# Gate/value stage of a three-part fp32 layer: five token groups of 464 or 448 columns in place of six of 384

## The chip, the cores and the metric

The kernel runs on one core of one Trainium2 chip. The metric is the device time of one execution in microseconds, the median of several runs. The core has five engines with an instruction stream each: PE (TensorE, matrix products), DVE (VectorE), ACT (ScalarE), POOL (GpSimd) and SP (SyncE, which here only issues transfers). They meet through semaphores alone.

## The reference

Chunked attention, a feed-forward layer with a softmax-weighted activation and a layer norm, and a gated feed-forward layer follow each other over 4608 tokens of 512 features. The change lies in the third one:

```python
def _moe2_ref(x, w_gate, w_val, w_out):      # x: 4608 x 512
    g = x @ w_gate                           # 512 x 1536
    silu = g * (1.0 / (1.0 + np.exp(-g)))
    val = x @ w_val                          # 512 x 1536
    return (silu * val @ w_out)              # 1536 x 512
```

## The kernel before

Each fp32 product is made of three passes over operands that are split into a high and a low part (`PASSES`: high x high, high x low, low x high). The products of the third layer also use a seven-product scheme for 2 x 2 blocks (Strassen's, in Winograd's form), so each operand is first turned into seven blocks, by differences and sums, and each block is split into high and low.

The program has three stretches. Up to 517 us it computes attention and the first feed-forward layer; its last part, called the y stage here, writes y (the input x of the code above) tile by tile to DRAM. An outer step m covers 384 tokens (`TOK`), d one of four feature tiles; one (m, d) is 24 matmuls of 384 columns (L169). Beside it `w_tick` prepares the seven factors of each of the 12 pairs of gate and value blocks and spills them to DRAM (`ws_dram`, 1792 KB each).

The gate/value stage (517 to 1042 us) has NSG = 6 groups s of two halves of 384 tokens. For each group, 12 steps f. A step (`step`) runs seven `product`s of six matmuls (two k tiles x three passes; L862), with a block of y as the moving operand of 384 columns and a 128 x 128 piece of a factor block as the stationary one. ACT, DVE and POOL empty the four accumulators, apply the sigmoid and form `u` = silu(gate) x value, and SP stores it to `u_dram` during the next step. The seven blocks of y for the next group (`yk`, two buffers, yka and ykb) are made while the present group runs: `y_load` fetches y into `rawy`, and `y_units` gives a list of 8 differences on POOL and 14 splits (one ACT copy, one DVE subtraction each), which is worked off in small portions. For group 0 the portions are three units at a time from y tile (10, 0) on. Factor blocks come through a ring of three buffers (`ring_tile`, `w_load`), always three ahead; blocks 0 to 2 are kept in cached copies (`wc`, `cache_load`) for the groups before the last, and the list `orders` tells which steps use them.

In the last two groups the output weights are made ready too: `v_load` to `v_store` convert them, then for each of six pairs p `t_load` fetches two rows of blocks, `t_sums` makes four differences on POOL, and `t_split` makes the split copy `tw[p]` (ACT, then DVE).

The output stage (1042 to 1314 us) runs NU = 54 units n = (g, p), 9 groups g of 512 tokens and six p. A unit has 2 x 21 matmuls of 256 columns (L1082). For unit n, `x_load` fetches u, `x_sums` makes four sums on DVE, `x_high` copies the high part on ACT into `hl[n]` (in the three-buffer ring), `x_low` makes the low part on DVE. Unit n needs `hl[n]` and `tw[p]`. After p = 5 `evac` empties the accumulators pa, pb, pc, pd of each half i: ACT copies pa, DVE adds pb, POOL adds, DVE adds pc, and so on. The next group's matmuls write the same banks.

The scheduler is switched off for all of this (`manual_schedule`): every engine runs its instructions strictly in the order in which the code issues them.

Of the kernel before, what the change touches and what calls it, by code (L numbers as in the profile page):

```python
# [23 lines left out]
def attn_moe_moe2_kernel(  # L24
# [38 lines left out]
    y_dram = [  # L63
        [dram.tile([P, TOK], F32, tag=f"y{m}_{d}", name=f"y{m}_{d}") for d in range(KD)]
        for m in range(NG)
    ]
# [94 lines left out]
    def y_run(wB, i0, i1, ps, sb, ptags=("y",), stag="ysb", queue=nc.scalar):  # L161

        for i in range(i0, i1):
# [9 lines left out]
            if n == NY - 1:  # L173
                ysb = sb.tile([P, TOK], F32, tag=stag, name="ysb", bufs=2)
                nc.scalar.activation(out=ysb, in_=ys.pop(u), func=AF.Copy)  # L175
                queue.dma_start(out=y_dram[m][d], in_=ysb)
# [61 lines left out]
    with ExitStack() as ph1:  # L238
# [459 lines left out]
    SG = 2 * TOK  # L698
    NSG = NG // 2
# [5 lines left out]
    u_dram = [  # L705
        [dram.tile([P, 2, SG], F32, tag=f"u{s}_{p}", name=f"u{s}_{p}") for p in range(NFP)]
        for s in range(NSG)
    ]

    with ExitStack() as ph2:  # L710
# [7 lines left out]
        ry = cpa.tile([P, 11, TOK], F32, tag="ry", name="ry")  # L718
        rawy, tt = ry[:, 0:8].rearrange("p (a b) n -> p a b n", a=2), ry[:, 8:11]
        yk = {0: cpa.tile([P, NS, 2, 2, TOK], F32R, tag="yka", name="yka")}  # L720
# [9 lines left out]
        def yk_tile(s):  # L730
            x = "ab"[s % 2]
            return (cpa, cp)[s % 2].tile([P, NS, 2, 2, TOK], F32R, tag=f"yk{x}", name=f"yk{x}")
# [18 lines left out]
        def y_load(s):  # L751
            for kk in range(2):
                for i, (m, k) in enumerate(((0, 0), (1, 0), (0, 2), (1, 2))):
                    nc.sync.dma_start(out=rawy[:, kk, i], in_=y_dram[2 * s + m][k + kk])

        def y_units(s, kks=(0, 1)):
# [3 lines left out]
            dst, units = yk[s], []  # L760
            for kk in kks:
                b11, b12, b21, b22 = (rawy[:, kk, i] for i in range(4))
                t1, t2, t4 = (tt[:, i] for i in range(3))
# [55 lines left out]
        for m in range(1, NG):  # L819
            for d in range(KD):  # L820
# [8 lines left out]
                if k == END:  # L829
                    ahead_y = y_units(0)  # L830
                if last_m and d == 0:
                    stage_.close()
                    p2.close()
                    cp = ph2.enter_context(pool("cp"))
                    for i in range(2):
                        osb = cp.tile([P, TOK], F32, tag="osb", name="osb", bufs=2)
                    yk[1] = yk_tile(1)
                if last_m and d < RING:
                    w_load()
                for x in ahead_y[:3]:  # L840
                    x()
                ahead_y = ahead_y[3:]
# [6 lines left out]
        def cache_load(f):  # L849
# [318 lines left out]
```

## Time and profile before

| | |
|---|---|
| median of 3 runs | 1322.7 us (1322.65 to 1322.89) |
| profiled execution, its own time | 1322.13 us |
| its span in the profile | 1320.3 us |
| PE busy | 1297.1 us (98%) |
| DVE, ACT, POOL busy | 995.9 (75%), 620.4 (47%), 449.9 (34%) us |
| granted clock of TensorE | 0.999 |

The profile lists instructions with their line in the kernel, what they write and read, how often they ran, and how long. A matmul's recorded duration is longer than the distance to the next one, since matmuls overlap; the distance is what counts. The letters x4 behind a row mean that four neighbours of one kind are merged, and the duration then runs from the first one's start to the last one's end. Square brackets tell how long the engine had been idle and what released it. SPq is SP's queue of transfers.

### The profile page before, as it was taken

The numbers are of one execution on the slowest core, as the hardware profiler recorded it, in microseconds if no ns is written. First come the engines' busy times: TensorE is split into PE (matmuls) and PEld (weight loads), VectorE is DVE, ScalarE is ACT, GpSimd is POOL, SyncE is SP. The second block draws the span as 40 slices with busy tenths as digits, with TensorE's granted clock in tenths as the row PEclk, the third lists the DMA queues.
The fourth block names the chain that finished last, engine by engine and source line by source line (L and its number), as shares of the span: only waits on it lengthen the run. The fifth ranks groups of instructions, "written<-read, shape, count | busy, mean of one in ns | idle before, by whom it ended". The sixth has DMA issues, their size and how long they took to land. (4 is left out here: it accounts for less than half of the span.)

```text
span 1320.3 us, 26319 instructions
## 1 busy us (share of the span) xinstructions
PE 1297.1 (98%) x10058; PEld 1242.3 (94%) x10058; DVE 995.9 (75%) x1674; ACT 620.4 (47%) x1024; POOL 449.9 (34%) x601
## 2 busy tenths in 40 slices
PE   4999999999999999999999999999999999999998
PEld 3788888888999999999999999999999999999998
DVE  7788888886478774687777777787777788787875
ACT  5566666666566654243333433343333333334331
POOL 5455555554333441243333333433432000000111
PEclk9999999999999999999999999999999999999999
DMA  7355556575799997997888798767999544444441
GB/s 256 121 177 177 177 178 183 183 212 179 268 369 357 395 334 288 411 423 237 284 274 312 246 326 277 275 209 275 346 340 342 176 146 142 144 129 144 128 150 60
DMA packets 146830, 318.40 MB, mean 241 GB/s; under 512 B 11536, under 2 KB 94480, under 8 KB 139024
## 3 DMA queue, kind: packets, MB, share of 16 engines
q1 hardware_dynamic: 140368, 308.07, 67.5%
q10 hardware_dynamic: 6336, 8.65, 1.8%
q8 instruction: 79, 1.29, 0.4%
q14 instruction: 47, 0.39, 0.1%
HBM read 225.45 MB, written 91.23 MB: 240 GB/s over the span
## 5 line engine op out<-in xcount | busy, mean ns | idle before, releaser
L381 PE MATMUL h<-wA,x 128*128 128x512 f32 x864 | 216.6, 399 | 0.6 <-ACT x L361 0.3
L169 PE MATMUL y<-lnT,wB 128*128 128x384 f32 x1152 | 200.7, 334 | 0.6 <-ACT ysb L175 0.6
L169 PEld LDWEIGHTS y<-lnT,wB 128*128 128x128 f32 x1152 | 199.5, 188 | 0.9 <-ACT ysb L175 0.9
L381 PEld LDWEIGHTS h<-wA,x 128*128 128x128 f32 x864 | 156.8, 188 | 32.1 <-ACT x L361 1.5
L895 POOL TENSOR_TENSOR u<-u,p 128x384 f32<-128x384 f32 x72 | 73.1, 1015 | 217.6 <-DVE u L894 217.6
L897 ACT ACTIVATE u<-pa 128x384 f32<-128x384 f32 x72 | 35.4, 492 | 176.0 <-PE pa L862 176.0
L1092 POOL TENSOR_TENSOR work<-work 128x256 f32<-128x256 f32 x35 | 25.8, 747 | 249.2 <-DVE work L1092 231.1
L1001 ACT ACTIVATE hl<-ry 128x1792 fp32r<-128x1792 f32 x28 | 47.7, 1703 | 78.6 <-PE opd L1082 42.6
L898 DVE TENSOR_TENSOR u<-pa,u 128x384 f32<-128x384 f32 x72 | 40.1, 558 | 58.6 <-ACT u L897 58.1
L902 ACT ACTIVATE u<-p 128x384 f32<-128x384 f32 x72 | 37.9, 526 | 94.9 <-DVE p L901 94.9
L1001 ACT ACTIVATE hl<-work 128x1792 fp32r<-128x1792 f32 x26 | 44.3, 1704 | 73.8 <-PE opd L1082 40.0
L862 PE MATMUL pd<-ykb,ws 128*128 128x384 f32 x360 | 72.2, 334 | 0.0
L862 PE MATMUL pc<-ykb,ws 128*128 128x384 f32 x360 | 72.1, 334 | 0.0
L862 PE MATMUL pa<-ykb,ws 128*128 128x384 f32 x360 | 72.1, 334 | 0.0
L668 DVE TENSOR_TENSOR lnT<-lr,lnT 128x1536 fp32r<-128x1536 f32 x24 | 47.5, 1978 | 31.5 <-ACT lnT L667 26.9
L1006 DVE TENSOR_TENSOR hl<-ry,hl 128x1792 fp32r<-128x1792 f32 x28 | 56.6, 2022 | 14.8 <-ACT hl L1001 14.8
L862 PE MATMUL pa<-yka,ws 128*128 128x384 f32 x324 | 64.8, 334 | 0.0
L862 PE MATMUL pc<-yka,ws 128*128 128x384 f32 x324 | 64.8, 334 | 0.0
L862 PE MATMUL pd<-yka,ws 128*128 128x384 f32 x324 | 64.8, 334 | 0.0
L1006 DVE TENSOR_TENSOR hl<-work,hl 128x1792 fp32r<-128x1792 f32 x26 | 52.6, 2022 | 15.8 <-ACT hl L1001 15.8
L862 PEld LDWEIGHTS pd<-ykb,ws 128*128 128x128 f32 x360 | 63.2, 188 | 0.2 <-DVE u L894 0.2
L361 ACT ACTIVATE x<-so_ps 128x512 fp32r<-128x512 f32 x36 | 21.7, 602 | 88.7 <-PE so_ps L265 84.4
(148 smaller groups left out, 3212.4 us busy)
## 6 DMA issues: line engine op xcount, KB each, us to landing
ws<-ws SPq DMA_DIRECT2D x57, 1792.0 KB, 9.1
u<-u SPq DMA_DIRECT2D x72, 384.0 KB, 7.2
ln<-lt SPq DMA_DIRECT2D x72, 256.0 KB, 3.1
lr<-ln SPq DMA_DIRECT2D x24, 768.0 KB, 7.1
ry<-u SPq DMA_DIRECT2D x56, 256.0 KB, 3.2
work<-u SPq DMA_DIRECT2D x52, 256.0 KB, 3.2
ws<-shi SPq DMA_DIRECT2D x12, 896.0 KB, 9.4
qt<-in_q SPq DMA_DIRECT2D x36, 256.0 KB, 3.6
```

Of the source, the lines that this page charges most:

```text
L169: nc.tensor.matmul(ys[u], lhsT=wB[:, f, a, d * P:(d + 1) * P], rhs=lnT[m][:, b, f, :], start=(n == 0), stop=(n == NY - 1),)
L361: nc.scalar.activation(out=hi, in_=o, func=AF.Copy)
L381: nc.tensor.matmul(h[:, n * DM:(n + 1) * DM], lhsT=x[:, a, k, :], rhs=wA[:, n * KD + k, b, :], start=(j == 0), stop=(j == NH // 2 - 1),)
L668: nc.vector.tensor_tensor(out=lo, in0=x, in1=hi.bitcast(F32), op=ALU.subtract)
L862: nc.tensor.matmul(ps, lhsT=w[:, a, kk * P:(kk + 1) * P], rhs=y[:, b, kk], start=(first and n == 0), stop=(n == 5), skip_group_check=True,)
L895: nc.gpsimd.tensor_tensor(out=u3, in0=u3, in1=p5, op=ALU.add)
L897: nc.scalar.activation(out=sa, in_=psA, func=AF.Sigmoid)
L898: nc.vector.tensor_tensor(out=sa, in0=psA, in1=sa, op=ALU.mult)
L902: nc.scalar.activation(out=sb, in_=c12, func=AF.Sigmoid)
L1001: nc.scalar.activation(out=hl[n][:, 0], in_=xs[n][:, 1:8], func=AF.Copy)
L1006: nc.vector.tensor_tensor(out=hl[n][:, 1], in0=xs.pop(n)[:, 1:8], in1=hl[n][:, 0].bitcast(F32), op=ALU.subtract,)
L1092: add = lambda eng, out, a, b: eng.tensor_tensor(out=out, in0=a, in1=b, op=ALU.add)
```

## The change

The five groups hold 2 x 464 tokens, the last 2 x 448 (`WIDTHS`); every tile and instruction of a step takes its width from the group. `y_dram` becomes one tensor per m and `u_dram` one per p, since a group's tokens no longer coincide with the pieces in which they are written and read. `y_load` therefore cuts each half at multiples of 384, and loads both k tiles in one transfer. The cached copies and the special orders go: all 60 factor blocks pass through the ring. Ring buffer 0 lies in pool `cp` as before, 1 and 2 lie in pool `cb`, which is opened after the last y tile. The differences of y get a tile of their own (`tt`); yka lies in a new pool `ka`, which is opened at y tile (11, 0), and all of group 0's `y_units` run from there, six at a time. `tw[0]` gets a buffer of its own, `tw[1]` to `tw[3]` use ykb's place, and `tw[4]` and `tw[5]` use a pool `kl` that takes yka's place when the gate/value stage is over; they are loaded, formed and split during the first units of the output stage (`prepare`). Evacuations use the tiles p1, p5 and u.

```diff
-    SG = 2 * TOK
-    NSG = NG // 2
+    WIDTHS = (464, 464, 464, 464, 448)
+    NSG = len(WIDTHS)
+    FIRST = [2 * sum(WIDTHS[:s]) for s in range(NSG)]
+    WM = max(WIDTHS)
...
-            tag = f"wsr{ring[0] % RING}"
+            i = ring[0] % RING
             ring[0] += 1
-            return cp.tile([P, NS, 2, HC], F32R, tag=tag, name=name)
-
-        stream = [(s, f) for s in range(NSG) for f in range(FT) if f >= RING or s == NSG - 1]
-        ahead = iter(stream)
-        ws, wc = {}, {}
+            return (cb if i else cp).tile([P, NS, 2, HC], F32R, tag=f"wsr{i}", name=name)
+
+        ahead = iter([(s, f) for s in range(NSG) for f in range(FT)])
+        ws = {}
...
-                if k == END:
-                    ahead_y = y_units(0)
                 if last_m and d == 0:
                     stage_.close()
                     p2.close()
                     cp = ph2.enter_context(pool("cp"))
+                    tt = cp.tile([P, 3, WM], F32, tag="tt", name="tt")
...
                     yk[1] = yk_tile(1)
-                if last_m and d < RING:
                     w_load()
...
+                    ka = ka_.enter_context(pool("ka"))
+                    ahead_y = y_units(0)
-                for x in ahead_y[:3]:
+                for x in ahead_y[:6]:
...
         cb = ph2.enter_context(tc.tile_pool(name="cb", bufs=1, reuse_waits="tile"))
+        w_load()
+        w_load()
...
         u_store()
         x_high(1)
         x_low(1)
 
-        work = cp.tile([P, 36, HT], F32, tag="ykb", name="work")
-        hold[0] = work[:, 0:16]
-        x_load(4)
-        x_load(5)
+        ka_.close()
+        kl = ph2.enter_context(pool("kl"))
+        t = kl.tile([P, 2, NS, 2, HC], F32R, tag="tw", name="tw")
+        t_home.update({4: t[:, 0], 5: t[:, 1]})
+        work = kl.tile([P, 2, 8, HT], F32, tag="work", name="work")
+        halves += [work[:, 0], work[:, 1]]
+        t_load(4)
+        t_load(5)
         x_sums(2)
         x_high(2)
         x_low(2)
-        x_sums(3)
+        t_sums(4)
+
+        def prepare(n):
+            if n in (1, 2):
+                x_sums(n + 2)
+                x_high(n + 2)
+                x_low(n + 2)
+                t_split(n + 3)
+                x_load(n + 5)
+                if n == 1:
+                    t_sums(5)
+            elif n:
+                if n == 3:
+                    x_sums(5)
+                x_high(n + 2)
+                x_sums(n + 3)
+                x_low(n + 2)
...
         for n in range(NU):
-            if n:
-                x_high(n + 2)
-                x_sums(n + 3)
-                x_low(n + 2)
+            prepare(n)
```

How the orders of the engines move is shown at three places. The first is DVE from the end of the gate/value stage into the output stage. A row `hl<-` is an `x_low`, a row of four with 128x256 is an `x_sums`, a row `tw<-` is the DVE half of a `t_split`. Before, from the low part of unit 1 on:

```order
L1006 TENSOR_TENSOR hl<-ry,hl 128x1792
L995 TENSOR_TENSOR ry<-ry 128x256 x4
L1006 TENSOR_TENSOR hl<-ry,hl 128x1792
L995 TENSOR_TENSOR ry<-ry 128x256 x4
L995 TENSOR_TENSOR work<-work 128x256 x4
L1006 TENSOR_TENSOR hl<-ry,hl 128x1792
L995 TENSOR_TENSOR work<-work 128x256 x4
L1006 TENSOR_TENSOR hl<-work,hl 128x1792
L995 TENSOR_TENSOR ry<-ry 128x256 x4
L1006 TENSOR_TENSOR hl<-work,hl 128x1792
```

The sums of unit 4 stand ahead of the low part of unit 3 there, and so on. The same place on DVE after the change, again from the low part of unit 1:

```order
L1001 TENSOR_TENSOR hl<-ry,hl 128x1792
L990 TENSOR_TENSOR ry<-ry 128x256 x4
L1001 TENSOR_TENSOR hl<-ry,hl 128x1792
L990 TENSOR_TENSOR ry<-ry 128x256 x4
L1001 TENSOR_TENSOR hl<-ry,hl 128x1792
L963 TENSOR_TENSOR tw<-work,tw 128x7x256
L990 TENSOR_TENSOR ry<-ry 128x256 x4
L1001 TENSOR_TENSOR hl<-ry,hl 128x1792
L963 TENSOR_TENSOR tw<-work,tw 128x7x256
L990 TENSOR_TENSOR ry<-ry 128x256 x4
L990 TENSOR_TENSOR work<-work 128x256 x4
L1001 TENSOR_TENSOR hl<-ry,hl 128x1792
```

Up to unit 4 the sums now stand directly ahead of the low part of the same unit, and two splits stand between; the old order is back with unit 5.

The second place is POOL at the same time: the last rows of the gate/value stage and the first behind it. Before:

```order
L895 TENSOR_TENSOR u_11903<-u_11903,p_11902 128x384
L895 TENSOR_TENSOR u_11974<-u_11974,p_11973 128x384
L895 TENSOR_TENSOR u_12044<-u_12044,p_12043 128x384
L895 TENSOR_TENSOR u_12113<-u_12113,p_12112 128x384
L1092 TENSOR_TENSOR work<-work 128x256 x35
```

Here the evacuation's additions (L1092) follow the stage at once. POOL after the change:

```order
L901 TENSOR_TENSOR u_11065<-u_11065,p_11064 128x448
L901 TENSOR_TENSOR u_11138<-u_11138,p_11137 128x448
L901 TENSOR_TENSOR u_11212<-u_11212,p_11211 128x448
L954 TENSOR_TENSOR work<-work 128x256 x8
L1103 TENSOR_TENSOR o<-o,p_11600 128x256 x2
```

Eight differences (L954, `t_sums` of p = 4 and 5) came in between, ahead of the evacuation.

The third place is SP's queue at the end of the y stage: a row `ws<-ws` fetches a factor block, a row `<-ysb` stores a y tile. Before:

```order
L234 DMA ws_141<-blk 128x1280
L749 DMA ws<-ws_133 128x3584
L176 DMA y_0_126<-ysb 128x384
L749 DMA ws<-ws_134 128x3584
L176 DMA y_1_127<-ysb 128x384
L749 DMA ws<-ws_135 128x3584
L176 DMA y_2_128<-ysb 128x384
L176 DMA y_3_129<-ysb 128x384
L749 DMA ws<-ws_136 128x3584
```

Three blocks are fetched between the stores. The same place after:

```order
L231 DMA ws_105<-blk 128x1280
L744 DMA ws<-ws_94 128x3584
L173 DMA y_93<-ysb 128x384 x4
L744 DMA ws<-ws_95 128x3584
L744 DMA ws<-ws_96 128x3584
L744 DMA ws<-ws_97 128x3584
```

The second and third block now stand behind all four stores.

## Rows read from the trace of the kernel before

**Rows 1.** Windows by stage: PE, PEld, DVE, ACT, POOL busy us, clock, DMA share, GB/s.

```profile
517.30:1041.70 524.40, 524.40 (x3026) 524.14 (x3025) 390.79 (x705) 197.08 (x415) 176.01 (x184) 1.00 0.83 297
1041.70:1314.20 272.50, 272.50 (x2264) 271.95 (x2264) 215.03 (x317) 100.33 (x72) 25.09 (x34) 1.00 0.42 134
```

**Rows 2.** Timeline of PE, output stage: start us, length us, engine, line, what, count.

```profile
1041.71 0.87 PE L1082 MATMUL opa<-tw,hl 128*128 128x256 f32 x6
...
1073.38 0.88 PE L1082 MATMUL opc<-tw,hl 128*128 128x256 f32 x6
```

**Rows 3.** Timeline of DVE, first units of the output stage.

```profile
1043.79 2.02 DVE L1006 TENSOR_TENSOR hl<-ry,hl 128x1792 fp32r<-128x1792 f32 x1
1045.72 1.55 DVE L995 TENSOR_TENSOR ry<-ry 128x256 f32<-128x256 f32 x4
1049.09 2.03 DVE L1006 TENSOR_TENSOR hl<-ry,hl 128x1792 fp32r<-128x1792 f32 x1 [1.82 <-ACT hl L1001]
...
1059.74 1.55 DVE L995 TENSOR_TENSOR ry<-ry 128x256 f32<-128x256 f32 x4
1061.21 2.02 DVE L1006 TENSOR_TENSOR hl<-work,hl 128x1792 fp32r<-128x1792 f32 x1
...
1070.83 0.68 DVE L1092 TENSOR_TENSOR work<-opb,work 128x512 f32<-128x512 f32 x1
1072.35 0.69 DVE L1092 TENSOR_TENSOR work<-opc,work 128x512 f32<-128x512 f32 x1 [0.84 <-POOL work L1092]
```

**Rows 4.** Timeline of ACT: the high part of unit 2.

```profile
1047.36 1.70 ACT L1001 ACTIVATE hl<-ry 128x1792 fp32r<-128x1792 f32 x1 [3.71 <-PE opd L1082]
```

**Rows 5.** Timeline of PE, hidden layer of the first network: 13 matmuls of 512 columns.

```profile
199.62 3.13 PE L381 MATMUL h<-wA,x 128*128 128x512 f32 x13
```

**Rows 6.** Timeline of PE where the gate/value stage begins.

```profile
517.32 1.20 PE L862 MATMUL pa<-yka,ws 128*128 128x384 f32 x6
```

**Rows 7.** Timeline of SP's queue there.

```profile
513.92 4.48 SPq L176 DMA_DIRECT2D y<-ysb  x2
```

**Rows 8.** Transfers issued in 524.7:525, then 532.7:533: KB, us from issue to landing.

```profile
ws<-ws SPq DMA_DIRECT2D x1, 1792.0 KB, 7.1
...
ws<-ws SPq DMA_DIRECT2D x1, 1792.0 KB, 9.4
```

**Rows 9.** Timeline of POOL, y stage: four differences of y.

```profile
484.54 6.82 POOL L767 TENSOR_TENSOR ry<-ry 128x384 f32<-128x384 f32 x4
```

**Rows 10.** Timeline of DVE, beside POOL's differences and alone.

```profile
488.06 2.42 DVE L668 TENSOR_TENSOR lnT<-lr,lnT 128x1536 fp32r<-128x1536 f32 x1 [2.13 <-ACT lnT L667]
...
493.35 1.76 DVE L668 TENSOR_TENSOR lnT<-lr,lnT 128x1536 fp32r<-128x1536 f32 x1
...
999.37 1.09 DVE L906 TENSOR_TENSOR u<-p,u 128x384 f32<-128x384 f32 x1
1000.38 0.55 DVE L907 TENSOR_TENSOR u<-u,u 128x384 f32<-128x384 f32 x1
1000.85 2.01 DVE L965 TENSOR_TENSOR twa<-ry,twa 128x1792 fp32r<-128x1792 f32 x1
...
1076.33 2.09 DVE L995 TENSOR_TENSOR work<-work 128x256 f32<-128x256 f32 x4
```

**Rows 11.** Timeline of POOL at two of those times.

```profile
996.79 3.26 POOL L954 TENSOR_TENSOR ry<-ry 128x256 f32<-128x256 f32 x4
...
1076.56 0.78 POOL L1092 TENSOR_TENSOR work<-work 128x256 f32<-128x256 f32 x1 [1.40 <-DVE work L1092]
```

**Rows 12.** Window of the end: columns as in rows 1.

```profile
1300.00:1320.30 20.30, 14.99 (x125) 14.78 (x124) 6.13 (x9) 2.86 (x3) 2.19 (x3) 0.96 0.14 52
```

**Rows 13.** Timeline of PE, first part: the same 32 matmuls at two times.

```profile
22.22 1.13 PE L265 MATMUL so_ps<-kt,qt 64*64 64x64 f32 x32
...
26.18 0.69 PE L265 MATMUL so_ps<-kt,qt 64*64 64x64 f32 x32
```

More of the change, by code (lines that the diff above doesn't have):

```diff
@@ L62, in attn_moe_moe2_kernel @@
     ln_dram = [dram.tile([P, KF, TOK], F32, tag=f"ln{m}", name=f"ln{m}") for m in range(NG)]
[L63 to L66, printed above, removed]
+    y_dram = [dram.tile([P, KD, TOK], F32, tag=f"y{m}", name=f"y{m}") for m in range(NG)]
     def wblock(pool, tag, n):
@@ L704, in attn_moe_moe2_kernel @@
     RING = 3
[L705 to L708, printed above, removed]
+    u_dram = [dram.tile([P, 2, NT * P], F32, tag=f"u{p}", name=f"u{p}") for p in range(NFP)]
     with ExitStack() as ph2:
@@ L751, in y_load @@
         def y_load(s):
-            for kk in range(2):
-                for i, (m, k) in enumerate(((0, 0), (1, 0), (0, 2), (1, 2))):
-                    nc.sync.dma_start(out=rawy[:, kk, i], in_=y_dram[2 * s + m][k + kk])
+            for i, (half, k) in enumerate(((0, 0), (1, 0), (0, 2), (1, 2))):
+                t, n = FIRST[s] + half * WIDTHS[s], 0
+                while n < WIDTHS[s]:
+                    m, o = divmod(t + n, TOK)
+                    c = min(TOK - o, WIDTHS[s] - n)
+                    nc.sync.dma_start(
+                        out=rawy[:, :, i, n:n + c], in_=y_dram[m][:, k:k + 2, o:o + c]
+                    )
+                    n += c
         def y_units(s, kks=(0, 1)):
@@ L759, in y_units @@
                 yk[s] = yk_tile(s)
-            dst, units = yk[s], []
+            w, units = WIDTHS[s], []
+            dst = yk[s][:, :, :, :, 0:w]
             for kk in kks:
-                b11, b12, b21, b22 = (rawy[:, kk, i] for i in range(4))
-                t1, t2, t4 = (tt[:, i] for i in range(3))
+                b11, b12, b21, b22 = (rawy[:, kk, i, 0:w] for i in range(4))
+                t1, t2, t4 = (tt[:, i, 0:w] for i in range(3))
                 t3 = b12
@@ L951, in t_sums @@
         def t_sums(p):
-            t4, b11, b21, t1, t2, t3, b22, b12 = (halves[p % 2][:, i] for i in range(8))
+            t4, b11, b21, t1, t2, t3, b22, b12 = (tx[p][:, i] for i in range(8))
             for o, a, b in ((t1, b12, b11), (t2, b22, t1), (t3, b22, b12), (t4, b21, t2)):
@@ L1048, in attn_moe_moe2_kernel @@
                 todo = todo[k:]
-                if 8 <= late < 8 + 2 * NFP and late % 2:
-                    t_split(late // 2 - 4)
-                if late in (20, 22):
-                    x_sums(late // 2 - 10)
+                if late in (15, 17, 19, 21):
+                    t_split(late // 2 - 7)
                 if late == 21:
+                    x_sums(0)
+                if late == 22:
                     x_high(0)
                     x_low(0)
+                    x_sums(1)
         u_store()
```

111 lines of the change are left out of this document (48 added, 63 removed).

## The prediction, on record before the run

> **What bounds the kernel now.** I read the windows by stage first, since the change touches two stages with different limits. In both PE is busy without a gap: 524.40 of 524.40 us in the gate/value stage, 272.50 of 272.50 in the output stage, at the 2.4 GHz level all the time [rows 1]. So there the time is the number of matmuls times the distance between two of them, as long as nothing leaves PE waiting. DVE comes next, with 390.8 us in the first and 215.0 in the second (79%). The second thing to read is therefore the timeline where the stages meet, because the change moves DVE work to exactly that place. The output stage starts at 1041.71; I call this zero. A unit lasts 42 x 0.120 = 5.04 us (272.50/2268 matmuls = 120.1 ns), so unit 2 starts at 10.1. DVE ends unit 2's low part at 1049.09 + 2.03 = 1051.12, which is 9.4 [rows 2, 3]. This is 0.7 us ahead of need: a just-in-time chain, hidden behind a busy PE. The chain is sums on DVE (1.55), 0.09 to ACT, the high part on ACT (1.70), 0.03 back, the low part on DVE (next instruction 1.93 later) [rows 3, 4].
>
> **Fewer matmuls.** Before, 6 x 12 x 42 = 3024 of 384 columns take 524.40, or 173.4 ns each [rows 1]. Against 120.1 ns for 256 columns that is 53.3 ns for 128 columns: 0.416 ns a column, and 13.6 ns that each matmul costs whatever its width. For 464 columns this gives 173.4 + 80 x 0.416 = 206.7 ns, for 448 200.0. After: 2016 x 206.7 + 504 x 200.0 = 416.7 + 100.8 = 517.5 us, a gain of 6.9. The other bound is a line between 384 and the 512-column row, (3.13 - 0.40)/12 = 228 ns [rows 5]: 207.2 and 200.5, a gain of 5.7. I take 6.9, since that line's 512-column row includes restarts behind other work. The wider evacuations lie beside PE (DVE 390.8 of 524.4 before, and fewer fixed costs after): nothing.
>
> **Streaming.** 60 factor blocks are fetched before (57 and 3 cached) and after, and one per step of 42 x 0.2067 = 8.68 us is no denser than before; each has two steps to land in. y pieces come a whole group early. Cost nothing; without that cover a load takes 7 to 9 us (below).
>
> **Start of the gate/value stage.** It starts at 517.32 [rows 6]. Blocks 1 and 2 now stand behind all four y stores on SP, and wait for the last y matmul. The fourth store ends at 513.92 + 4.48 = 518.40 [rows 7], so block 1 is issued 1.1 us into the stage and needed at 8.68. A load on idle queues landed after 7.1, one that others followed at once after 9.4 [rows 8]: 8.2 or 10.5, a wait of 0 or 1.8 us. The first row is the nearer one, with idle queues as here; with the y store just ahead of it I take 0.3. Queued behind the wait are block 2, needed at 17.4, and later ones. The y factors of group 0 are the other thing squeezed here: eight differences and fourteen splits now fit into the four last y tiles, 96 x 0.1734 = 16.6 us. Four differences of 384 columns with DVE work between them took 6.82 [rows 9]; eight of 464 take 2 x 6.82 x 464/384 = 16.5. They can start a few us into this time, when the ground is free, and end some 4 us into the stage, while the last is wanted by the seventh product at 7.4: nothing, with 1.5 as upper bound for an early product.
>
> **Start of the output stage.** Here the splits of two weight pairs and eight POOL differences come in. DVE's chain after the change, from zero: the low part of unit 1 starts at 2.08 before; four additions of 64 columns more each make it 2.3. Then 1.93 (low 1) = 4.2. Units 2, 3 and 4 each take 1.55 + 0.09 + 1.70 + 0.03 + 1.93 = 5.30, because their own sums now stand right before the low part and DVE idles while ACT copies: 20.1. Two splits of 1792 elements (2.01 [rows 10], so 1.93 to the next): 24.0. Sums 5, with sums 6 inside the wait for ACT, until low 5 starts: 3.37, so 27.4. Low 5, sums 7, low 6, sums 8, low 7: 1.93 + 1.47 + 1.93 + 1.47 + 1.95, so 36.1. Then the evacuation of group 0, until the addition from pc ends: 1072.35 + 0.69 - 1070.83 = 2.2, so 38.3. Unit 6's first matmul into pc overwrites that bank and would start at 1073.38 - 1041.71 = 31.7 [rows 2, 3]. It is **6.6 us late**. Before, the same addition ended 0.3 us early. The lateness appears in parts (at unit 4's third matmul already), but only the end counts, since nothing in the chain waits for PE. Afterwards DVE needs about 4 us of every 5 and the lead comes back.
>
> **POOL beside DVE.** The chain above has DVE alone. DVE additions with both inputs in SBUF were slowed beside POOL: 1.09 us while four POOL differences ran, 0.55 alone; four sums 2.09 instead of 1.55 beside one POOL addition; a long subtraction 2.42 instead of 1.76 [rows 3, 10, 11]. I read this as taking turns: whichever comes second waits for the other's instruction. One POOL difference lasts (3.26 - 0.47)/4 = 0.70, the 0.47 being the DVE instruction let through (1000.38 to 1000.85). The first four start when `t_load(4)` has landed, at about 9, and meet sums 3: four turns, 2.8. Of the other four, two fall into DVE's wait for ACT, one holds low 3 by 0.3, and one holds the split by 0.7. Together **3.8**, between 0 (all fall into DVE's idle time) and 8 x 0.70 = 5.6. I take 3.8 since the row of four sums beside POOL is the same instruction as the one that is met.
>
> The Trainium skill, on the page "SBUF — State Buffer" (section "SBUF: two separate sides"), states the like for a DVE instruction with two SBUF inputs against a POOL instruction that reads SBUF: one port pair, held for the whole instruction. By that rule the order put the differences where they hurt, and the sum with it is 1326.5; were it not so here, it would be 1322.7. The rows above agree with the rule.
>
> **Sum.** The profiled execution took 1322.13 us (span 1320.3). 1322.13 - 6.9 + 0.3 + 6.6 + 3.8 = 1325.9. The median of the runs is 0.57 higher: **1326.5**.
>
> **Rivals.** (1) POOL's differences fall into DVE's idle time: the chain costs 6.6 alone, 1322.13 - 6.9 + 0.3 + 6.6 + 0.57 = 1322.7. For it: DVE idles three times 1.8 us there. Against: a four-row POOL sequence met DVE work and held it in each of the cited rows. (2) The output stage absorbs the splits, and the change is faster: DVE has 57 us free there, the low part of unit 5 ended at 1061.21 + 2.02, some 3.9 us before unit 5 wanted it at 1067.1 [rows 3], and two splits cost 2 x 1.93 = 3.9. If ACT's copies did not stop DVE, that lead would just do: 1322.7 - 6.9 + 0.3 = 1316.1. It decides if the sums of the next unit are ready early enough; against it, the order has sums, copy and low part back to back. (3) The start of the gate/value stage waits 1.8 us instead of 0.3: 1328.0. (4) PE's pauses lower its clock. It was at 0.96 on average in the last window, where PE had ended 6 us before the span did [rows 12]; and early in the program, after pauses, 32 matmuls took 1.13 us that took 0.69 later [rows 13]. A unit at the 1.2 GHz level lasts 42 x 256 x 0.416 ns = 4.5 us more; three such units hide some of the DVE chain, and by the positions above unit 6's pc would come about 4 us later: 1330.5. Against it, the pauses are only 2 to 3 us long, with matmuls between. The skill's page "TensorE: Matmul & The Clock Gate" (section "Why this matters for your kernels") advises against idle gaps between bursts for this reason; no row shows pauses of this length in mid-program. (5) The change does not do what it says: a matmul's cost grows in proportion, 173.4 x 464/384 = 209.5 ns. Then the gain of 6.9 is gone, 1333.4; the line through two widths speaks against it.
>
> **Chances.** The forecast with its bounds (POOL between 2 and 5.6, the matmul gain between 5.7 and 6.9: 1324.7 to 1329.5) 0.54; rival 1 0.22; rival 2 0.11; rival 3 0.05; rival 4 0.05; rival 5 0.03. The range leaves out rivals 2, 4 and 5: 1321.9 (rival 1 with a chain 0.8 us shorter) to 1329.5. About 0.2%, 2.6 us, is what a measurement of this kernel can tell from no change: faster is below 1320.1, slower above 1325.3. Faster: rival 2, 0.11. Same: rival 1 and the part of the forecast where POOL costs under 2.6, 0.22 + 0.10 = 0.32. Slower: 0.57.
>
> **What would show it.** The gate/value stage should last 517.5 us with PE busy throughout and matmuls 206.7 ns apart; 520 or more would be step one wrong. A PE pause of over 1 us at its second step means the late block. In the first 45 us of the output stage PE should lose about 10 us: waits for DVE before units 3, 4 and 5, then before pb and pc of unit 6. If these pauses come to 7, the turns with POOL were overpriced; if to none, the chain was; `x_sums` of unit 3 should take about 4 us instead of 1.55. A granted clock below 1.00 there is rival 4.

## Result and profile of the kernel after

The kernel after took **1332.96 us** (median of 6 runs, 1331.66 to 1333.39) against 1322.68 for the kernel before (6 runs): a ratio of 1.0078, 95% interval 1.0065 to 1.0091. It is slower, as forecast, but by 10.3 us instead of 3.8; 1332.96 lies above the range. The profiled execution took 1333.1 us, its span 1331.3.

Windows by stage, columns as in [rows 1], which has the first stage of the kernel before (524.40). First its output stage, cut at the last matmul, and then both stages of the kernel after, cut in the same way:

```profile
1041.71:1314.83 273.12, 273.12 (x2269) 272.53 (x2268) 215.54 (x317) 100.32 (x72) 25.13 (x35) 1.00 0.42 133
```

```profile
517.90:1041.80 523.90, 523.90 (x2521) 472.99 (x2521) 367.88 (x593) 184.83 (x350) 162.02 (x156) 1.00 0.87 300
1041.80:1325.90 284.10, 276.60 (x2269) 274.15 (x2267) 223.25 (x320) 103.67 (x74) 34.75 (x43) 0.99 0.42 132
```

The first number after the window is its length, the next is PE's busy time. The gate/value stage issues 504 matmuls fewer and gains 524.40 - 523.90 = 0.5 us, not 6.9. PE is busy in all of it, so this is no wait: the matmuls themselves are further apart. The output stage is 11.0 us longer. PE is idle there for 284.10 - 276.60 = 7.5 us, and its busy time grew by 3.5 us though it does the same 2268 matmuls.

The same view of the kernel after by group (four of 464 tokens a half, the last of 448):

```profile
517.90:622.60 104.70, 104.70 (x505) 94.56 (x505) 68.54 (x110) 36.67 (x70) 30.05 (x27) 1.00 0.88 312
622.60:728.00 105.40, 105.40 (x505) 94.42 (x504) 75.54 (x122) 37.32 (x75) 33.97 (x32) 1.00 0.90 304
...
938.30:1041.80 103.50, 103.50 (x506) 94.84 (x505) 72.96 (x117) 36.17 (x59) 30.42 (x33) 1.00 0.79 276
```

Divided by 504 matmuls this is 207.7 ns in the first group, 209.1 in the second and 205.4 in the last, where the line of the prediction gave 206.7 and 200.0. Groups 2 and 3 repeat the first two (104.80 and 105.50).

PE's waits in the first 58 us of the output stage of the kernel after (who waits, for what: us in all, times, longest):

```profile
PE opa L1092 <- DVE hl L1001: 2.8, 3, 1.6
PE opa L1092 <- ACT hl L996: 2.4, 1, 2.4
PE opb L1092 <- DVE o L1103: 1.7, 1, 1.7
PE opc L1092 <- DVE o L1103: 0.6, 1, 0.6
```

`hl` are the input factors of a unit, `o` the evacuation of group 0. These four rows are the 7.5 us, at the places that the prediction named. The timeline of DVE there answers [rows 3]; the last row is POOL's:

```profile
1051.89 1.97 DVE L990 TENSOR_TENSOR ry<-ry 128x256 f32<-128x256 f32 x4
1055.76 2.23 DVE L1001 TENSOR_TENSOR hl<-ry,hl 128x1792 fp32r<-128x1792 f32 x1 [1.90 <-ACT hl L996]
1057.91 2.55 DVE L963 TENSOR_TENSOR tw<-work,tw 128x1792 fp32r<-128x1792 f32 x1
1060.38 3.17 DVE L990 TENSOR_TENSOR ry<-ry 128x256 f32<-128x256 f32 x4
1065.44 2.03 DVE L1001 TENSOR_TENSOR hl<-ry,hl 128x1792 fp32r<-128x1792 f32 x1 [1.89 <-ACT hl L996]
...
1053.96 8.86 POOL L954 TENSOR_TENSOR work<-work 128x256 f32<-128x256 f32 x7 [0.38 <-DMA work<-wo]
```

The chain is the forecast one: behind the low part of unit 2 come the sums of unit 3, 1.90 us of waiting for ACT, low part, with a split of 2.55 (alone 2.02) before the sums of unit 4. The four instructions at 1051.89 to 1060.38 are longer than their like (1.55, 2.02, 2.02, 1.55) while POOL makes its eight differences, 2.8 us together.

About 3.0 of the 3.5 us of extra busy time stand in the clock. Two stretches of the kernel after, columns as above:

```profile
1067.60:1071.00 3.40, 3.40 (x16) 3.40 (x17) 3.37 (x6) 0.00 (x0) 0.00 (x0) 0.50 0.53 157
1084.70:1088.00 3.30, 3.30 (x18) 3.30 (x17) 2.19 (x5) 0.00 (x0) 1.90 (x3) 0.50 0.66 244
```

The granted clock is 0.50, the 1.2 GHz level: 16 matmuls of 256 columns take 3.40 us, 0.21 each instead of 0.12, which is 1.5 us more in each stretch. The rows of PE just ahead show what it did before: two pauses with two matmuls between them ahead of the first stretch, and the two waits for the evacuation ahead of the second.

```profile
1065.46 0.51 PE L1092 MATMUL opa<-tw,hl 128*128 128x256 f32 x2 [2.37 <-ACT hl L996]
1067.52 1.21 PE L1092 MATMUL opa<-tw,hl 128*128 128x256 f32 x4 [1.55 <-DVE hl L1001]
...
1082.25 0.98 PE L1092 MATMUL opb<-tw,hl 128*128 128x256 f32 x6 [1.72 <-DVE o L1103]
1083.80 0.98 PE L1092 MATMUL opc<-tw,hl 128*128 128x256 f32 x6 [0.57 <-DVE o L1103]
```

The last row is the matmul that the prediction asks for, unit 6's first into pc. It starts 1083.80 - 1041.80 = 42.0 us into the stage, 10.3 later than before (31.7); the prediction wanted 10.4. The first stretch at the lower clock lies inside this delay: PE comes to its next operands earlier than DVE even so, and DVE's rows up to there show no wait for PE. Only the second one lies behind it.

### The profile page after: what moved, and what is told of

Same layout as the page of the kernel before. It is cut to its first block, busy times and chain, and to the rows that moved or that the text cites. A ratio compares the mean times of both kernels' runs of the same rounds, so it can differ in the third digit from the quotient of the medians.

```text
span 1331.3 us, 24975 instructions
## 1 busy us (share of the span) xinstructions
PE 1300.7 (98%) x9554; PEld 1193.2 (90%) x9554; DVE 981.4 (74%) x1564; ACT 612.1 (46%) x962; POOL 449.2 (34%) x581
## 4 chain that ended last, share of the span: by engine, by line
PE 94%; DVE 3%; issue 1%; ACT 1%; DMA 0%; POOL 0%; SPq 0%; POOLq 0%; ACTq 0%; DVEq 0%
PE y L166 15%; PE h L378 15%; PE pd L866 11%; PE pa L866 11%; PE pc L866 11%; PE pb L866 6%; PE opc L1092 5%; PE opa L1092 5%; PE opb L1092 5%; PE so_ps L262 3%; PE tr L459 3%; PE opd L1092 3%; PE pt L332 1%; DVE hl L1001 1%; ACT hl L996 1%
## 5 line engine op out<-in xcount | busy, mean ns | idle before, releaser
L378 PE MATMUL h<-wA,x 128*128 128x512 f32 x864 | 216.7, 399 | 0.6 <-ACT x L358 0.3
L166 PE MATMUL y<-lnT,wB 128*128 128x384 f32 x1152 | 200.7, 334 | 0.6 <-ACT ysb L172 0.6
L1092 PE MATMUL opa<-tw,hl 128*128 128x256 f32 x648 | 96.8, 285 | 5.2 <-DVE hl L1001 2.8
L866 PE MATMUL pd<-yka,ws 128*128 128x464 f32 (+1 forms) x432 | 101.1, 369 | 0.0
L866 PE MATMUL pa<-yka,ws 128*128 128x464 f32 (+1 forms) x432 | 101.0, 369 | 0.0
L866 PE MATMUL pc<-yka,ws 128*128 128x464 f32 (+1 forms) x432 | 101.0, 369 | 0.0
L1092 PE MATMUL opb<-tw,hl 128*128 128x256 f32 x648 | 96.1, 284 | 1.7 <-DVE o L1103 1.7
L1092 PE MATMUL opc<-tw,hl 128*128 128x256 f32 x648 | 96.2, 284 | 0.6 <-DVE o L1103 0.6
L1092 PEld LDWEIGHTS opa<-tw,hl 128*128 128x128 f32 x648 | 86.2, 192 | 6.1 <-DVE hl L1001 3.5
L866 PEld LDWEIGHTS pc<-yka,ws 128*128 128x128 f32 x432 | 81.1, 188 | 8.2
L1092 PEld LDWEIGHTS opb<-tw,hl 128*128 128x128 f32 x648 | 86.2, 193 | 1.9 <-DVE o L1103 1.9
L1092 PEld LDWEIGHTS opc<-tw,hl 128*128 128x128 f32 x648 | 85.6, 192 | 1.9 <-DVE o L1103 1.9
```

The lines of the kernel that those rows point to most:

```text
L166: nc.tensor.matmul(ys[u], lhsT=wB[:, f, a, d * P:(d + 1) * P], rhs=lnT[m][:, b, f, :], start=(n == 0), stop=(n == NY - 1),)
L378: nc.tensor.matmul(h[:, n * DM:(n + 1) * DM], lhsT=x[:, a, k, :], rhs=wA[:, n * KD + k, b, :], start=(j == 0), stop=(j == NH // 2 - 1),)
L866: nc.tensor.matmul(ps, lhsT=w[:, a, kk * P:(kk + 1) * P], rhs=y[:, b, kk], start=(first and n == 0), stop=(n == 5), skip_group_check=True,)
L1092: nc.tensor.matmul(acc[g, i, t][:, half], lhsT=hl[n][:, a, j, i * P:(i + 1) * P], rhs=tw[p][:, j, b], start=(p == x == half == 0), stop=(p ...
```

## Experiments

Two questions: why 464 columns cost more than the line says, and what the 11 us of the output stage are made of. "Stage" times of variants are cut like those above.

**The matmul alone: start of the rows, or their number?** In the kernel before, a row of the moving operand was 384 floats (1536 bytes); after, it is 464 (1856 bytes), so the starts of the streamed rows changed with the width. This kernel streams matmuls with nothing beside them:

```
for k in range(n):
    nc.tensor.matmul(acc, lhsT=wt[:, a, kk * P:(kk + 1) * P], rhs=y[:, o:o + w], ...)
```

> This kernel leaves the whole computation out and writes zeros; it only issues matmuls without a pause, in blocks of 84 (126 for a pattern), each block into a PSUM tile whose name says its shape: w = so many columns from the start of one buffer; m0 to m128 = 464 columns from a start shifted by so many floats; n0 to n64 = the same with 384 columns; pA_B = A columns, and the starts step through the rows of a buffer of pitch B floats in the order of the kernel after (rows 0, 2, 0, 1, 3, 1 of each product); tight = 464 columns into a PSUM tile of 464 instead of 512. Theory A (the start of the streamed rows counts): w464 takes 206.7 ns, some shifted starts and p464_464 take up to 212, p464_512 206.7, and 384 columns at shifted starts and p384_464 take more than 173.4. Theory W (the number of columns counts): w464 is already 207.9 or more, all starts and patterns of one width are equal, 384 stays at 173.4 everywhere, and the line 13.6 + 0.416 ns a column fails at 448, 464, 480 alike. Theory S (the PSUM tile counts): tight differs from w464, nothing else.

Windows that hold one block each. First 464 columns: start 0 floats and 48 floats (84 matmuls each), the pattern of the kernel after at pitch 464 and at pitch 512 (126 each), a PSUM tile of 464 (84); then 384 columns: start 32 floats (84), pattern at pitch 464 (126).

```profile
260.81:278.46 17.65, 17.65 (x86) 15.74 (x85) 0.00 (x0) 0.60 (x1) 0.00 (x0) 1.00 0.01 1
349.35:367.25 17.90, 17.90 (x85) 15.71 (x84) 0.00 (x0) 0.56 (x1) 0.00 (x0) 1.00 0.00 0
460.83:487.21 26.38, 26.38 (x128) 23.65 (x128) 0.00 (x0) 0.49 (x1) 0.00 (x0) 1.00 0.00 1
513.60:539.91 26.31, 26.31 (x127) 23.66 (x126) 0.00 (x0) 0.56 (x1) 0.00 (x0) 1.00 0.00 1
682.17:699.71 17.54, 17.54 (x85) 15.78 (x85) 0.00 (x0) 0.49 (x1) 0.00 (x0) 1.00 0.00 1
...
431.49:446.26 14.77, 14.77 (x85) 14.77 (x85) 0.00 (x0) 0.49 (x1) 0.00 (x0) 1.00 0.01 1
660.33:682.17 21.84, 21.84 (x128) 21.84 (x128) 0.00 (x0) 0.49 (x1) 0.00 (x0) 1.00 0.00 1
```

Per matmul 464 columns take 210.1, 213.1, 209.4, 208.8 and 208.8 ns: never 206.7, with a spread of 4 ns by the start. 384 columns take 175.8 and 173.3. Theory A falls, since 464 columns cost 2 ns more than the line at every start that was tried. Theory W is not whole either, since the start adds up to 4 ns on top. The smaller PSUM tile is worth 1.3 ns at most (208.8 against 210.1 from the same start).

**The same in the kernel.**

```diff
-            return (cp if s % 2 else ka).tile([P, NS, 2, 2, WM], F32R, ...)
+            return (cp if s % 2 else ka).tile([P, NS, 2, 2, DM], F32R, ...)
```

The weight-decoding buffers and the factors of pair 0 were moved to make room.

> The kernel after with y factors in rows of 512 floats instead of 464 (the first 464 or 448 of each are used), and the weight factors of pair 0 in the y buffer beside those of pairs 1 to 3. Theory A (start of the streamed rows): matmuls 206.7 and 200.0 ns apart without a pattern, gate/value stage 517.5 us instead of 523.9, total 1326.5. Theory W (number of columns): stage 523.9, matmuls 207.9 on average as in the kernel after, total 1333.

1331.76 us (1331.69 to 1331.94; ratio 1.0071, 1.0056 to 1.0086). The stage takes 523.68 us. Its first two groups and its last:

```profile
517.94:623.78 105.84, 105.84 (x505) 94.61 (x505) 68.47 (x110) 36.82 (x70) 30.02 (x27) 1.00 0.87 309
623.78:729.05 105.27, 105.27 (x505) 94.66 (x504) 75.54 (x122) 37.45 (x75) 33.88 (x32) 1.00 0.88 304
...
940.17:1041.62 101.45, 101.16 (x505) 94.33 (x505) 73.06 (x117) 35.80 (x59) 30.68 (x33) 1.00 0.80 281
```

464 columns stay at 208.9 to 210.0 ns in rows of 512. 448 columns fell from 205.4 to 200.7 (PE busy, 101.16/504), nearly the line. For that width something other than the number of columns counts; the pitch alone it is not, since in rows of 512 the stream above took 202.7 and the next one 206.6.

**Which widths?** The stream again, in the order of the stage (six matmuls into one PSUM tile, other weights for each six), 126 of each width.

> Again a kernel that leaves the computation out and writes zeros. Matmuls without a pause, now in the order of the gate/value stage (six into one PSUM tile, then the next of pa, pc, pb, pd, pa, pc, pd; other weights for each six), 126 of each width. Names: s = that many columns from rows of pitch 512 floats, q = rows as long as the width, f = all from one start, o448 = one set of weights. From the first stream: 256, 384 and 512 columns took 119.9, 173.3 and 226.8 ns, on one line (13.3 + 0.4167 a column); 448, 464, 480 and 496 took 202.7 to 206.7, 208.8 to 213.3, 216.6 and 223.3, which is 2 to 7 ns above it. Theory W128 (only multiples of 128 columns lie on the line): 288, 320, 352, 400, 416, 432, 440, 448, 456, 464, 480 and 496 all lie 2 ns or more above, whatever the pitch. Theory W64 (multiples of 64 do): 320 and 448 lie on it at pitch 512 (133.3+13.3 = 146.7 and 200.0), as in the stage of the kernel with pitch 512, where 448 columns took 8.40 us for 42. Theory N (the excess comes only above 384 columns): 288, 320 and 352 lie on the line.

Blocks of 384, 400, 416, 448, 464 and 512 columns (length, PE, then PEld, the weight loads); the table has three more widths:

```profile
164.93:186.77 21.84, 21.84 (x127) 21.84 (x127) 0.00 (x0) 5.88 (x12) 0.00 (x0) 1.00 0.00 1
186.77:209.45 22.68, 22.68 (x127) 22.68 (x127) 0.00 (x0) 6.06 (x12) 0.00 (x0) 1.00 0.00 1
209.45:233.18 23.73, 23.73 (x128) 23.60 (x128) 0.00 (x0) 6.19 (x12) 0.00 (x0) 1.00 0.00 1
...
283.06:309.09 26.03, 26.03 (x127) 23.65 (x126) 0.00 (x0) 6.54 (x12) 0.00 (x0) 1.00 0.00 1
335.39:361.72 26.33, 26.33 (x128) 23.66 (x126) 0.00 (x0) 6.69 (x12) 0.00 (x0) 1.00 0.00 1
...
417.16:445.74 28.58, 28.58 (x127) 23.66 (x126) 0.00 (x0) 7.16 (x12) 0.00 (x0) 1.00 0.00 1
```

| columns | 384 | 400 | 416 | 432 | 448 | 464 | 480 | 496 | 512 |
|---|---|---|---|---|---|---|---|---|---|
| measured, length/126, ns | 173.3 | 180.0 | 188.3 | 195.9 | 206.6 | 209.0 | 216.7 | 223.3 | 226.8 |
| 13.3 + 0.4167 a column | 173.3 | 180.0 | 186.7 | 193.3 | 200.0 | 206.7 | 213.3 | 220.0 | 226.7 |

288 to 352 lie on the line too, or 1.6 ns under it (288). So the line holds up to 400 columns and again at 512, and between them a matmul costs 2 to 7 ns more. Theory N comes nearest; the "multiples" theories fall with 288, 352 and 400, and with 448.

The page "TensorE: Matmul & The Clock Gate" of the Trainium skill (section "Back-to-back issue gap") gives N/2.4 + 2.5 ns for an isolated matmul, by which 195.8 ns would be the estimate for 464 columns. These rows, of a stream with a weight load for each matmul, differ, and the measurement decides: here the constant is 13.3, and one line does not cover all widths.

**Is the weight load behind it?** In the table the excess begins where the spacing passes the 188 ns that a weight load lasts in the trace. Narrower weights make the load shorter.

> A kernel that leaves the computation out and writes zeros; matmul streams as in the second one, 84 of each. cA_B = B columns against weights of A columns (64 or 96 instead of 128), s = 128 columns of weights at further widths. In the second stream a weight load lasted 187.5 ns, and the excess over the line 13.3 + 0.4167 ns a column began between 400 columns (a matmul every 180.0 ns) and 416 (186.7 by the line, 188.4 measured), was 2 to 7 ns from there to 496 and nothing at 512. Theory L (the excess appears where the weight load is done before the matmul is): with 64 columns of weights the load is shorter, and the excess begins at narrower widths than 400, in proportion at about 200. Theory C (it is the column count of the moving operand alone): 416, 448, 464 and 480 show their excess with 64 and 96 columns of weights too, 288, 320 and 384 none. In both, 504 and 508 tell whether 512 alone is free of it.

With 64 columns of weights, blocks of 384, 416, 448 and 512 columns, 84 each:

```profile
135.11:149.67 14.56, 14.56 (x87) 11.33 (x84) 0.00 (x0) 3.81 (x8) 0.00 (x0) 1.00 0.01 2
149.67:165.49 15.82, 15.82 (x85) 11.31 (x84) 0.00 (x0) 4.06 (x8) 0.00 (x0) 1.00 0.00 1
165.49:182.48 16.99, 16.99 (x85) 11.25 (x84) 0.00 (x0) 4.27 (x8) 0.00 (x0) 1.00 0.00 0
...
218.42:237.76 19.34, 19.34 (x85) 11.33 (x84) 0.00 (x0) 4.71 (x8) 0.00 (x0) 1.00 0.00 0
```

173.3, 188.3, 202.3 and 230.2 ns. The loads (PEld, 11.3 us of the block) now last 135 ns each, and the excess still begins above 384: theory L falls. 512 is not free of it with these weights (3.5 ns over). Theory C, the width of the moving operand alone, does not hold as it stands either: with 96 columns of weights 384 took 174.9, 1.6 over the line, and 416 took 186.8, on it. With 128 columns of weights 408 took 185.0 (1.7 over), and 504 and 508 took 226.9 and 227.7, 3.6 and 2.7 over. What makes the excess stays open.

**Other widths, the same work.** If width is the cause, groups of 256, 384 and 512 with as many matmuls and columns must give the 517.5 us that the prediction wanted.

```diff
-    WIDTHS = (464, 464, 464, 464, 448)
+    WIDTHS = (256, 512, 512, 512, 512)
...
```

> The kernel after with rows of 512 floats, and the same tokens in groups of 256, 512, 512, 512 and 512 instead of 464 (448): as many matmuls and as many columns, so the line 13.3 + 0.4167 a column gives the same 517.5 us for the stage as the prediction did. Theory W128: each step 5.04 or 9.52 us, the stage 12 x 42 x (119.9 + 4 x 226.8) ns = 517.7, total 1326 with the output stage of the kernel after. Rival (the excess comes from the stage itself: weights, PSUM or other engines beside it): about 524 again, total 1332.

1343.84 us. From the second group on the stage is as expected, 456.99 us for 48 steps without a pause, 226.7 ns a matmul:

```profile
594.60:1051.59 456.99, 456.99 (x2019) 378.38 (x2018) 321.86 (x484) 158.86 (x281) 141.18 (x130) 1.00 0.82 282
```

But the first, narrow group (12 steps of 5.04 us, 60.5 together) took 77.0, with PE waiting 7.3 us for factor blocks, 3.1 for DVE and 0.9 for ACT, and its clock at 0.96: new waits, not the width. So once more with 384 in place of 256:

```diff
-    WIDTHS = (464, 464, 464, 464, 448)
+    WIDTHS = (384, 512, 512, 512, 384)
...
```

> The kernel after with rows of 512 floats and groups of 384, 512, 512, 512 and 384 tokens: the same 2520 matmuls and the same columns as the kernel after. By the widths measured alone (173.3 and 226.7 ns): stage 504 x (2 x 173.3 + 3 x 226.7) ns = 517.4 us instead of 523.9, total 1326 to 1327, if the first, narrower group does not stall as the one of 256 did (its steps are 7.28 us instead of 5.04). Rival (the stage adds the excess whatever the widths): 524, total 1332. Rival (the 512-token factors cannot be made in 12 steps of 7.28): waits for ACT and DVE in the first group, total over 1329.

1330.95 us (ratio 1.0064, 1.0050 to 1.0078). The gate/value stage:

```profile
517.75:1039.45 521.70, 518.89 (x2521) 458.51 (x2521) 372.81 (x599) 184.76 (x351) 164.58 (x156) 1.00 0.86 302
```

PE's busy time in the stage is 518.9, within 1.5 of the 517.4 worked out from the widths, where the variant with rows of 512 and the old widths had its PE busy for nearly all of 523.68. The stage itself lasts 2.8 more: PE waited 1.0 for the second factor block, 0.5 for ACT and 1.3 for DVE in the shorter steps.

**What the output stage lost.** Without pairs 4 and 5:

```diff
...
-        t_load(4)
-        t_load(5)
...
-        t_sums(4)
...
-                t_split(n + 3)
...
-                    t_sums(5)
...
-                        rhs=tw[p][:, j, b],
+                        rhs=tw[p if p < 4 else p - 2][:, j, b],
```

> The kernel after without the loads, differences and splits of weight pairs 4 and 5; their matmuls read the factors of pairs 2 and 3, so that part of the result is another. Both theories of the output stage agree here: 8 to 11 us come back (output stage 273 to 276 us instead of 284.1, total 1322 to 1325) if the splits on DVE and POOL's differences make the whole loss. What stays is the chain of sums, high and low parts in a row (about 2.8 us by the prediction's chain). If the stage stays over 280, something else is late there.

1328.34 us (1327.0 to 1330.05), 4.6 less than the kernel after; output stage 279.03. Both theories had hoped for 273 to 276. And without POOL's differences alone:

```diff
...
-        t_sums(4)
...
-                    t_sums(5)
...
+                nc.sync.dma_start(out=dst, in_=wo_dram[2 * p + j]...)   # into the rows of the differences
```

> The kernel after without the eight POOL differences of weight pairs 4 and 5; the rows that they made are loaded instead (the same blocks a second time), so that part of the result is another. The splits on DVE and ACT stay. Theory of the prediction (POOL and DVE take turns on the chain): the output stage gets 3.8 us shorter, 280.3, total 1329. Rival (POOL falls into DVE's idle time): nothing changes, 284 and 1333.

1331.12 us (1329.58 to 1332.76), 1.8 less than the kernel after; output stage 280.91. The profiled execution is the fastest of the four runs, and the median lies only 0.6 under that of the variant with rows of 512, which does the same output work as the kernel after. So the totals do not settle what POOL costs; the positions in the traces say more. Both output stages, without pairs 4 and 5 and then without POOL's differences:

```profile
1042.16:1321.19 279.03, 275.84 (x2269) 274.21 (x2267) 216.62 (x318) 100.42 (x72) 25.11 (x35) 0.99 0.41 131
```

```profile
1041.30:1322.21 280.91, 275.31 (x2269) 272.69 (x2267) 220.36 (x320) 103.66 (x74) 25.10 (x35) 0.99 0.43 138
```

In these two, and in the variant with rows of 512 (output stage 282.85), only one stretch at the 1.2 GHz level stands instead of two. Without pairs 4 and 5 it comes behind unit 6's first matmul into pc, where it costs time; in the other two it comes ahead of it, as the first one does in the kernel after. So the lengths of the stages cannot be subtracted from one another. What can be compared is the start of that matmul, which DVE's chain sets. With rows of 512, without POOL's differences, without pairs 4 and 5:

```profile
1083.56 0.98 PE L1087 MATMUL opc<-tw,hl 128*128 128x256 f32 x6 [0.57 <-DVE o L1098]
```

```profile
1081.31 0.98 PE L1094 MATMUL opc<-tw,hl 128*128 128x256 f32 x6 [0.56 <-DVE o L1105]
```

```profile
1078.20 1.58 PE L1084 MATMUL opc<-tw,hl 128*128 128x256 f32 x6 [0.56 <-DVE o L1095]
```

| kernel | before, and last version | no pairs 4, 5 | no POOL differences | rows of 512 | after |
|---|---|---|---|---|---|
| pc of unit 6, us into the stage | 31.67 | 36.04 | 40.01 | 41.94 | 42.00 |

The steps between the columns are 4.4 for the order (sums, high part and low part of a unit in a row), 4.0 for the splits and 1.9 for POOL. Two of the variants bring a wait of their own, though. Without POOL's differences the first split waits for its ACT copy, and that waits 1.08 us for the blocks that are loaded in their place (the bracket names another load that landed last):

```profile
1057.59 2.02 DVE L963 TENSOR_TENSOR tw<-work,tw 128x1792 fp32r<-128x1792 f32 x1 [0.76 <-DMA ry<-u]
1059.53 1.54 DVE L990 TENSOR_TENSOR ry<-ry 128x256 f32<-128x256 f32 x4
1062.97 2.03 DVE L1001 TENSOR_TENSOR hl<-ry,hl 128x1792 fp32r<-128x1792 f32 x1 [1.89 <-ACT hl L996]
```

Without pairs 4 and 5 the sums of unit 7 wait 0.64 us for a load of u. Put right for these two, the order costs 3.7, the splits 3.9 (two of 1.94) and POOL 2.7 us. In the 3.7 are 0.8 by which the low part of unit 1 starts later (2.83 us into the stage instead of 2.08). POOL's 2.7 agrees with the 2.8 by which the four DVE instructions grew: with POOL silent the sums of unit 4 took 1.54 us instead of 3.17. What the order does shows in DVE's wait for ACT ahead of the low part, here without pairs 4 and 5 (low part of unit 4) and then in the last version below, which has the order of before (low part of unit 3):

```profile
1061.06 2.02 DVE L1001 TENSOR_TENSOR hl<-ry,hl 128x1792 fp32r<-128x1792 f32 x1 [1.89 <-ACT hl L996]
```

```profile
1049.16 2.02 DVE L1014 TENSOR_TENSOR hl<-ry,hl 128x1792 fp32r<-128x1792 f32 x1 [0.17 <-ACT hl L1009]
```

**A version from these findings.** Widths on the line, no splits in the output stage, and its order of before (high part, sums of the next unit, low part). The first try:

> Groups of 512, 512, 512, 512 and 256 tokens, and the factors of all six weight pairs made in the gate/value stage: the y factors of the last, narrow group fill half of their buffer, and pairs 0 and 1 go into the other half during group 3, pairs 2 to 5 into the other y buffer during group 4. The output stage has no splits and takes the order of the kernel before. Theory (width, then the splits): stage 517.7, output stage 273 to 276, total 1316 to 1319. Rival (the last group is too short, 60 us, for its splits and sums): waits on DVE in the last steps, total over 1320.

1326.22 us (ratio 1.0029, 1.0017 to 1.0041). The output stage is back at 273.31 us and the four wide groups take 457.29; the last group of 256 took 69.48 instead of 60.5, with waits of 3.7 us for DVE, 2.1 for ACT and 1.0 for a factor block. The rival was right.

> Groups of 384, 512, 512, 512 and 384; the factors of all six weight pairs made in the gate/value stage. The y factors of the narrow groups leave a quarter of their buffer free: pair 0 goes there and pair 5 into the buffers of the y differences and of the weight decoding during group 3, pairs 1 to 4 into the other y buffer during group 4; the decoding of the output weights runs twice as fast in groups 1 and 2, so that it is done by then. The output stage has the order of the kernel before. Theory: stage 517.4, output stage 273, total 1322.7 - 7.0 = 1315.7 and 0.6 either way. Rival (the last group, 7.28 us a step, is held up by its four splits as the one of 256 was): 1318 or more.

1323.72 us (1322.19 to 1327.23; ratio 1.0012, 1.0003 to 1.0021). In the profiled execution (1326.57) the last group runs freely, but PE waited twice for ACT, 4.8 us in all, in the second step of groups 1 and 2, each time with the lower clock behind it (0.83 over the 10 us). ACT in group 1:

```profile
623.28 0.43 ACT L80 ACTIVATE vv<-vv 128x256 f32<-128x256 f32 x1 [6.17 <-DMA wo<-vv]
623.62 0.41 ACT L86 ACTIVATE vv<-vv 128x256 int32<-128x256 uint32 x1
623.94 0.58 ACT L915 ACTIVATE p<-pa 128x512 f32<-128x512 f32 x1
```

The weight decoding (L80, L86) stands ahead of the copy from PSUM (L915) for which PE waits, and it waits itself for the store of decoded weights (`wo<-vv`), which SP had issued only at 617.43, behind eight y loads that held its queue for 8.84 us. The third version lets the decoding pause there, and begins with the wide groups:

```diff
-    WIDTHS = (384, 512, 512, 512, 384)
+    WIDTHS = (512, 512, 512, 384, 384)
...
-                vs = list(islice(vq, (n > 2, 2, 2, 0, 0)[s]))
+                vs = list(islice(vq, (n > 2 if s == 0 else 2 * (n > 1)) if s < 4 else 0))
```

> As the version with 384, 512, 512, 512 and 384, with two things changed. The groups are 512, 512, 512, 384 and 384, so that the first step lasts 9.5 us and its second factor block (8.5 us after the start of the stage) comes in time; pair 1 goes into the free quarter of one y buffer in group 2, pairs 0 and 5 are made in group 3, pairs 2 to 4 in group 4. And the decoding of the output weights pauses in the first two steps of groups 1, 2 and 3, where its load stood behind the eight y loads on SP, ACT waited for it and PE for ACT (4 us and 4.6 us in the second steps of groups 1 and 2, with matmuls at 0.427 us for some 4 us behind them). Theory: stage 504 x (3 x 226.7 + 2 x 173.3) ns = 517.4, output stage 273.2, total 1315.7. Rival: the stalls were something else and stay, total 1322 or more.

**1317.48 us** (5 runs, 1316.96 to 1318.11) against 1322.51: ratio 0.9963, interval 0.9950 to 0.9977. It beats both kernels. The waits for ACT are gone, but the order of the groups changed with the pause, so what the pause alone is worth was not tried. Its stages:

```profile
517.52:1036.40 518.88, 518.04 (x2521) 458.52 (x2521) 365.50 (x595) 186.82 (x353) 165.78 (x164) 1.00 0.85 304
1036.40:1309.63 273.23, 273.23 (x2269) 272.52 (x2268) 215.54 (x317) 100.45 (x72) 25.14 (x35) 1.00 0.42 135
```

The gate/value stage gains 5.5 us on the kernel before, and the output stage is as long as there (273.12). The total is 1.8 above the 1315.7 of the theory, 1.5 of it in the gate/value stage.

## Why the prediction failed, step by step

- **Fewer matmuls** is the step that failed. It drew a line through 256 and 384 columns (0.416 ns a column and 13.6 ns) and read 206.7 and 200.0 ns off it; the stage shows 207.7 to 209.1 and 205.4, and a gain of 0.5 us instead of 6.9. The line is right where it was measured: 512 columns lie on it as well. But the rows that the prediction had, at 256, 384 and 512, all lie outside the stretch of widths where it does not hold. Its second bound (5.7) came from the same kind of row and could not show it. The prediction's own mark for it (a stage of 520 us or more) was met with 523.90. At the widths 384 and 512 the gain is there: 5.5 us in the last version. Why the widths between cost more is open. (The window of [rows 1] that was divided by 2268 matmuls holds 2264 of them; this moves the 206.7 by 0.1 only.)
- **Rival 5** came out near the total (1333.4) by its number, not by its reason, which is luck: a cost in proportion would make 512 columns 173.4 x 512/384 = 231.2 ns, and they take 226.8.
- **Start of the gate/value stage**, 0.3: nothing was lost; PE is busy in all 523.90 us. It was close: in the variant with a first step of 7.28 us PE did wait 1.0 us for the second block.
- **Start of the output stage**, 6.6 + 3.8 = 10.4: the mechanism held, and unit 6's first matmul into pc came 10.3 later than before. That the number is so close is partly luck. The chain without POOL cost 3.7 + 3.9 = 7.6 instead of 6.6, among other things since the low part of unit 1 began 2.84 us into the stage instead of 2.3; POOL cost 2.7 instead of 3.8. The prediction's own mark for this ("if these pauses come to 7, the turns with POOL were overpriced") points the right way with its 7.5, but the 7.5 leave out what PE lost inside the same delay at the lower clock. The stage as a whole is 11.0 longer: behind that matmul it lasts 242.10 us instead of 241.45. In the variant with rows of 512, which lacks the second stretch at the lower clock, it lasts 240.91, so that stretch costs some 1.2; why the rest is 0.5 shorter than before is not shown.
- **Turns of POOL and DVE.** The mechanism held, so rival 1 (all of it falls into DVE's idle time) falls. The place was another one than forecast: POOL began 10.9 us into the stage instead of 9, the sums of unit 3 took 1.97 us instead of some 4, and the sums of unit 4 took most of it (3.17 beside POOL, 1.54 without). The Trainium skill, page "SBUF — State Buffer", section "SBUF: two separate sides", has DVE and POOL share one port pair. The trace agrees with it, by the 3.17 us against 1.54.
- **Order and splits** cost nearly the same, 3.7 and 3.9 us. Rival 2 (the splits are absorbed) was wrong for the reason that the prediction had given against it: with sums, high part and low part of each unit in a row, DVE stands idle for 1.89 us while ACT copies, and the lead that would have taken up the splits is gone. In the last version, which has the order of before, the wait ahead of unit 3 is 0.17, but no split is left in that stage; the splits with the old order were not tried.
- **Rival 4**, the lower clock, got 0.05 and partly happened, beside the forecast and not instead of it. It was priced by whole units at the 1.2 GHz level; two stretches of 3.4 us came. The first was hidden in PE's waiting for the chain, and the second cost some 1.2 us.

The sum with the measured parts: 1322.13 + 0.6 (the stage starts at 517.90 instead of 517.32) - 0.5 + 11.0 = 1333.2, against 1333.1 profiled. The 0.6 need not belong to the change: in the two variants that differ from the kernel after in the output stage alone the same point lies at 518.25 and 517.39.

## What to carry over

A line through two widths does not vouch for a third: stream the very shape of matmul that is planned, by itself, before a stage is rebuilt around it. Fewer and wider matmuls pay here with groups of 384 and 512 columns and not with 464. When a variant takes a piece of work out, look whether it brings a wait of its own before its time is subtracted. Work that is moved to where two stages meet is priced by the chain of the engine that prepares the next operands, in its order, and a pause of PE can cost again through its clock.

## What was not expected of the hardware

- Matmuls with 128 columns of fp32r weights follow 13.3 + 0.4167 ns a column from 320 to 400 columns and at 256 and 512. From 408 to 508 they cost 2 to 7 ns more, 6.6 at 448. The setting moves this by some ns: 448 columns took 200.7 and 205.4 in the two kernels and 202.7 to 206.6 in the streams, 464 columns 208.8 to 213.1 by the start of the rows. The cause is open.
- With 128 columns of weights, 128, 192 and 224 columns all took 111 to 112 ns (9.33, 9.41 and 9.39 us for 84); the weight loads fill these blocks.
- In mid-program the granted clock fell to 0.50 for some 3.4 us after two PE pauses close together (2.37 and 1.55 us; 1.72 and 0.57), though PE had been busy for hundreds of us before. It did not always: in the variant with rows of 512 the second pair (1.89 and 0.57) left it at 1.00.
